# DeltaNet and a PReLU feed-forward block on one core: the opening with masked 16x16 blocks, half the columns, and values in three rounds

## The chip, the cores and the metric

The kernel runs on one core of one Trainium2 chip. The metric is device time in microseconds from the start to the end of one execution. Engines are called PE (TensorE), DVE (VectorE), ACT (ScalarE), POOL (GpSimd) and SP (SyncE, which here only issues loads and stores; its queue of them is SPq in the profile).

## The reference

Two blocks follow each other. The first is a delta rule over 768 tokens, for 4 batches and 8 heads of 48 dimensions, in float32:

```python
k_n = k / (norm(k) + 1e-06)
state = zeros((B, H, D, D))
for t in range(S):
    y[t] = q[t] @ state
    v_old = k_n[t] @ state
    state = state + beta[t] * outer(k_n[t], v[t] - v_old)
```

Its output, with the heads side by side as 3072 rows of 384, goes through the second block:

```python
h = x @ w_in                                   # 384 -> 2048
g = maximum(h, 0) + alpha * minimum(h, 0)
out = g @ w_out                                # 2048 -> 384
```

## The kernel before

The tokens are cut into 12 chunks of 64 (`C`). A step `n` is one chunk of one pair of batches, so there are 24 steps; steps 0 and 1 are chunk 0, steps 2 and 3 chunk 1. The 128 partitions of a step hold the 64 tokens of two batches. Inside a chunk the recurrence is a triangular system: with the weighted Gram matrix of the keys A (strictly lower), the values wanted are (I + A)^-1 times the values that the state leaves.

Most steps get that inverse from `eliminate`, which works on four steps (`NJ`) together with 32x32 blocks. The first four steps would wait too long for it. They use `eliminate_small`: it inverts only the 16x16 diagonal blocks (width `LB`, half of `HB`) on DVE, 14 dependent pairs of products and additions. What stands outside these blocks (`beyond`) is put in by a product: with own inverse D and outside part B, M = -DB is nilpotent (its fourth power is zero), so the inverse is (I + M)(I + M^2) D.

The opening of the program is, in this order, for steps 0 to 3:

- `squared`, `norms`: squares on ACT, sums on DVE. `flipped` (L412): keys turned by PE, copied by ACT to `k_t`.
- `grams` (L464): 16 products of 64x64 for each step; DVE multiplies them by the weights (L470) into three tiles: the columns of the own half (`same`), the other half (`right`), and `beyond` for steps 0 and 1. `keep` copies the second 32 rows; `outside` (L623 to L626) masks what stands outside the 16x16 blocks on ACT.
- `betas`, `slopes`: beta and alpha turned by PE (L316, L335). Alpha is loaded as `al_sb`; its slot is that of `prod`, which `eliminate_small` uses.
- `queries` (L1481): scores of q and k for chunk 0, masked by DVE (L1489).
- `short` and `busy` (L1474, L1466): matmuls whose results nobody reads; `busy(9)` runs beside the elimination. It reads `k_late[0]` (`kl`), the keys that the state update of step 0 also reads.
- `first_chunk`: `place_small` lays the inverses into 64x64 tiles (`own_inverse`); `matrices` makes M and its transpose and adds the identity (`eye`); `squared_matrix` M^2; three factors (L784 for all of these) give the values; then `outputs` (L857), `to_ffn` (L896: the outputs turned into the feed-forward block's operand).

The weights come in through a conversion of their own. `fetch_in` lets SP load pieces of w_in (128x512) into spare tiles (`stages`); `begin_in` runs two ACT instructions on a piece (L227, L229); `convert` adds one on DVE (L243) and one on POOL (L250). A piece's matmuls wait for the last.

`second_pair` does steps 2 and 3. Their products stand between the first-layer matmuls of chunk 0 (`ffn_in`, L995): `alongside(products, pieces)` puts so many of these matmuls and so many conversion halves behind a burst. Here `next_state` (L873) updates the state and `through_state` (L741, L729) reads it.

The order on each engine is written out by hand: `manual_schedule` keeps the order in which the program issues instructions, so an instruction that waits holds all behind it on its engine. SP's loads and stores go out in the order of the program as well. `hold` is a load of 4 bytes that makes SP wait for a tile. PSUM is shared out as three pairs of banks in turn (`ps_big`) and two banks for the feed-forward block (`ps_ffn`).

Of the kernel before, what the change touches and what calls it, by code (L numbers as in the profile page):

```python
# [32 lines left out]
C = 64  # L33
HB = 32
W_IN_P = 512
BUSY = 9.0
# [7 lines left out]
def kernel(  # L44
# [227 lines left out]
    eye = const.tile([128, C], FP32, name="eye")  # L272
    for t in range(2):
        nc.gpsimd.tensor_copy(out=minus[half(t)], in_=upper[half(t), half(t)])
    for t in range(2):
        nc.gpsimd.tensor_copy(out=eye[half(t)], in_=ident[half(t), half(t)])

    ones = work.tile([128, HB, HB], FP32, name="ones", tag="turned", bufs=1)
    nc.gpsimd.memset(ones, 0.0)
    nc.gpsimd.affine_select(  # L280
        out=ones, in_=ones, compare_op=ALU.is_ge, fill=1.0, base=0,
        pattern=[[1, HB], [-1, HB]], channel_multiplier=0,
    )
    inside_ = const.tile([128, HB * (HB + 1)], S8, name="inside")
    inside = inside_[:, 0 : HB * HB].rearrange("p (r c) -> p r c", c=HB)
# [3 lines left out]
    for t in range(2):  # L289
# [3 lines left out]
    first_of = const.tile([128, 1], FP32, name="first_of")  # L293
    nc.vector.tensor_reduce(
        out=first_of, in_=ident.rearrange("p (q u e) -> p u q e", u=2, e=HB // 2)[:, 0],
        axis=mybir.AxisListType.XY, op=ALU.add,
    )


    below = const.tile([128, 2], FP32, name="below")  # L300
    nc.gpsimd.tensor_tensor(out=below, in0=which, in1=first_of.to_broadcast([128, 2]), op=ALU.mult)
    nc.gpsimd.tensor_scalar(
        out=below[:, 0:1], in0=below[:, 0:1], scalar1=-1.0, scalar2=1.0, op0=ALU.mult, op1=ALU.add
    )
    nc.gpsimd.tensor_tensor(
        out=below[:, 1:2], in0=which[:, 1:2], in1=below[:, 1:2], op=ALU.subtract
# [42 lines left out]
    def zeros():  # L349

        for t in state:
            nc.scalar.memzero(t)

# [13 lines left out]
    ksq = {}  # L367

# [4 lines left out]
    def norms(n):  # L373
        stats[n] = work.tile([128, H], FP32, name="norm", bufs=EARLY + 3)
        nc.vector.tensor_reduce(out=stats[n], in_=ksq.pop(n), axis=AXX, op=ALU.add)  # L375
# [82 lines left out]
    def grams(n, p=None):  # L458

        if n >= N:  # L460
            return []
        p = region(p, G * C, g=G)
        for g, a, t in quarters():
            nc.tensor.matmul(  # L464
                p[half(t), a, g], k_t[n][dims(a), g, half(t)], k_t[n][dims(a), g, half(t)]
            )

        def weighted(dst, cols):
            w = stats[n][1][:, 0:2, :, None].to_broadcast([128, 2, G, HB])
            nc.vector.tensor_tensor(  # L470
                out=dst.rearrange("p (a g) i -> p a g i", a=2), in0=p[:, :, :, cols], in1=w,
                op=ALU.mult,
            )

        if n >= NJ:
            return [
                lambda: weighted(gather(n), slice(0, HB)),
                lambda: weighted(right[n % EARLY][:, 1:], slice(HB, C)),
                lambda: keep(n),
            ]  # L480
        return [
            lambda: weighted(gather(n), slice(0, HB)),
            lambda: weighted(right[n][:, 1:], slice(HB, C)),
            lambda: keep(n),
            lambda: weighted(beyond[n][:, :, 0:HB], slice(0, HB)),
        ]
# [13 lines left out]
    small = {}  # L500
    LB = HB // 2

    def own_blocks(flat):

        x = flat.rearrange("p (s e) -> p s e", s=2)[:, :, 0 : HB * LB]
        return x.rearrange("p s (r c) -> p s r c", c=HB)[:, :, :, 0:LB]

# [6 lines left out]
    def keep(n):  # L514

        m, j = n // NJ, n % NJ
        for t in range(2):
            own = slice(64 * t + HB, 64 * t + C)
            if n < FIRST + NJ and n != NJ - 1:
                nc.gpsimd.tensor_copy(out=same[m][own, j], in_=right[n % EARLY][own, 1:])  # L520
            elif n < NJ and t == 0:
                nc.vector.tensor_copy(out=same[m][own, j], in_=right[n % EARLY][own, 1:])
            else:
                nc.scalar.copy(same[m][own, j], right[n % EARLY][own, 1:])
        if (m, j) == (0, NJ - 1):
            for _ in turn_in(m):
                pass
# [11 lines left out]
    def turn_in(m):  # L539
        flat = work.tile([128, HB * (HB + 1)], FP32, name="block", bufs=1)  # L540
        block[m] = flat[:, 0 : HB * HB].rearrange("p (r c) -> p r c", c=HB)
        small[m] = own_blocks(flat)
        yield from turns(
            lambda x: block[m][:, x] if m == 0 else block[m][:, :, x].rearrange("b r c -> b c r"),
# [3 lines left out]
    def eliminate(m):  # L548

        if m > 0:  # L550
            yield from turn_in(m)
# [23 lines left out]
    def back(m):  # L575

        r = block[m]
        if m > 0:
            turned[m] = work.tile([128, NJ * H, HB], FP32, name="turned", bufs=1)
            yield from turns(  # L580
                lambda x: turned[m][:, :, x].rearrange("c b r -> c r b"), lambda x: r[:, x]
            )
# [10 lines left out]
    def eliminate_small(m):  # L593
        x = small[m]
        nc.vector.tensor_tensor(out=x, in0=x, in1=own_blocks(inside_), op=ALU.mult)
        yield
        for j in range(1, LB - 1):
# [12 lines left out]
            if j == 1:  # L610

                nc.gpsimd.memset(block[m][:, 0:LB, LB:HB], 0.0)
                nc.gpsimd.memset(block[m][:, LB:HB, 0:LB], 0.0)
                nc.gpsimd.memset(block[m].rearrange("p r c -> p (r c)")[:, :: HB + 1], 1.0)
            yield
        yield from back(m)

    def outside(n, part):

        x, left, last = beyond[n], beyond[n][:, :, 0:HB], right[n][:, 1:, 0:LB]  # L620
        if part == 0:
            src = left if n < 2 else same[0][:, n]
            nc.scalar.mul(left[:, :, 0:LB], src[:, :, 0:LB], below[:, 0:1])  # L623
            nc.scalar.mul(left[:, :, LB:HB], src[:, :, LB:HB], which[:, 1:2])
        else:
            nc.scalar.mul(x[:, :, HB : HB + LB], last, below[:, 1:2])  # L626
# [4 lines left out]
    def whole_block(out, x, i, by_vector=False):  # L631

        cols = slice(HB * i, HB * i + HB)
        if by_vector:
            nc.vector.tensor_scalar(
                out=out[:, :, cols], in0=x, scalar1=which[:, i : i + 1], scalar2=None, op0=ALU.mult
            )
        else:
            nc.scalar.mul(out[:, :, cols], x, which[:, i : i + 1])

    def place_small(n, by_vector):

        for i in range(2):
            whole_block(own_inverse[n], inverse[0][:, n * H : n * H + H], i, by_vector)
# [90 lines left out]
    def through_state(n, p=None, p_y=None):  # L735
# [9 lines left out]

        r = work.tile([128, 2, G, D], FP32, name="r")
# [3 lines left out]
        def less(to, own, a):  # L750
# [8 lines left out]
            *([lambda: weigh_rest_side(n)] if n < NJ else []),  # L759
# [4 lines left out]
    def weigh_rest_side(n):  # L764
        w = stats[n][1][:, 0:2, :, None].to_broadcast([128, 2, G, D])
        nc.vector.tensor_tensor(out=rhs_[n], in0=rhs_[n], in1=w, op=ALU.mult)

    def scale_first(n):
        c, bp = steps[n]
        nv[n] = v_raw.pop(n)  # L770
        nc.gpsimd.tensor_tensor(
            out=nv[n], in0=nv[n], in1=beta_t[:, c, bp, :, None].to_broadcast([128, H, D]),
            op=ALU.mult,
        )
        rhs_[n] = by_parity(nv[n])
# [4 lines left out]
    def crossing(out, x, y, back):  # L780

        for g, a, t in quarters():
            rows, own = (half(t ^ a), half(t)) if back else (half(t), half(t ^ a))
            nc.tensor.matmul(out[own, a, g], x[rows, a, g], y[rows, a, g])  # L784

    powers = {}

    def matrices(n, p=None):

        p = ps_big() if p is None else p  # L790
        one, other = (region(p[:, :, i * G * C : (i + 1) * G * C], G * C, g=G) for i in range(2))
        x, y = heads(own_inverse[n]), heads(beyond[n])
# [1167 lines left out]
```

## Time and profile before

| | us |
|---|---|
| median of 3 runs | 664.11 (663.17 to 664.46) |
| the profiled execution | 665.38 |
| its span, first to last instruction | 663.6 |
| PE: first instruction | 4.47 |
| DVE: the 14 steps of the small elimination | 19.85 to 27.64 |
| PE: first product of M | 31.09 |
| PE: first matmul of the feed-forward block | 47.92 |

Busy time of the engines in stretches of the opening (us, columns PE, weight loads, DVE, ACT, POOL each with the number of instructions, the granted clock of PE, the share of the DMA engines, GB/s):

```profile
20.00:30.00 10.00, 10.00 (x56) 4.81 (x49) 8.98 (x33) 7.86 (x18) 0.02 (x1) 1.00 1.07 340
30.00:40.00 10.00, 6.85 (x338) 5.47 (x336) 5.98 (x14) 4.54 (x9) 1.30 (x1) 1.00 0.63 113
40.00:50.00 10.00, 8.59 (x203) 7.27 (x203) 2.49 (x7) 6.18 (x13) 2.60 (x2) 0.83 0.57 170
```

A busy PE in the first of these is the filler. How to read a timeline line below: start, duration, engine, line of the kernel, operation, written tile and read tiles, shape, number of instructions; in brackets the idle time before it and what ended it. One float32 matmul of the program is two in the trace.

### The profile page before, as it was taken

The page shows a single profiled execution, that of the slowest core. Times are in us where ns is not written, and L with a number is a line of the kernel's source. Part 1 is how long each engine was busy: PE and PEld are TensorE (multiplying, and loading weights), DVE is VectorE, ACT ScalarE, POOL GpSimd, SP SyncE. Part 2 cuts the span into 40 slices and gives each one's busy share as a digit, 9 for nine tenths or more (in the row PEclk, how much of TensorE's full clock was granted, in tenths as well). Part 3 has the DMA queues.
Part 4 walks back from the last instruction along what each step waited for, and adds up shares of the span by engine and source line. Part 5 has one row for each costly group of instructions (what it writes and reads, how often), then busy time and mean ns, then how long its engine had stood idle before and what let it go on. Part 6 is the DMA issues. An engine that isn't in the chain of part 4 may idle for free.

```text
span 663.6 us, 21688 instructions
## 1 busy us (share of the span) xinstructions
PE 641.1 (97%) x9305; PEld 565.4 (85%) x9305; DVE 486.3 (73%) x1144; ACT 265.3 (40%) x620; POOL 124.6 (19%) x238
## 2 busy tenths in 40 slices
PE   6977998999999999999999999999999999999997
PEld 5566777656688988998998998988999999999997
DVE  4847479987899879758859748858968658568383
ACT  5755666424554252243343242232135235042140
POOL 6023554410010100001000000000035044052250
PEclk9989899999999999999999999999999999999999
DMA  7966555211342122122112112112111210100000
GB/s 118 290 151 126 154 140 134 74 36 29 65 80 50 27 52 46 26 49 50 26 38 37 27 38 37 26 39 37 26 41 35 41 34 3 28 11 2 25 0 25
DMA packets 111157, 37.68 MB, mean 57 GB/s; under 512 B 104230, under 2 KB 107446, under 8 KB 111062
## 3 DMA queue, kind: packets, MB, share of 16 engines
q1 hardware_dynamic: 109190, 35.81, 24.9%
q8 instruction: 73, 1.20, 0.7%
q10 hardware_dynamic: 1872, 0.49, 0.4%
q14 instruction: 22, 0.18, 0.1%
HBM read 31.56 MB, written 4.72 MB: 55 GB/s over the span
## 4 chain that ended last, share of the span: by engine, by line
PE 87%; DVE 7%; ACT 3%; issue 2%; DMA 1%; POOL 0%; SPq 0%; DVEq 0%; POOLq 0%; ACTq 0%
PE p_ffn L995 22%; PE p_ffn L1060 17%; PE p_more L1312 8%; PE p_ffn L1038 5%; PE p_more L1228 4%; PE p_ffn L1218 3%; PE p_ffn L1312 3%; PE p_ffn L1223 2%; PE p_pair L412 2%; PE p_pair L681 2%; PE p_pair L741 2%; PE p_pair L857 2%; PE p_pair L464 2%; PE p_pair L844 2%; PE p_pair L1466 2%
## 5 line engine op out<-in xcount | busy, mean ns | idle before, releaser
L995 PE MATMUL p_ffn<-xt,w_in 128*128 128x256 f32 x768 | 177.9, 385 | 3.2 <-DVE sums L1007 1.6
L995 PEld LDWEIGHTS p_ffn<-xt,w_in 128*128 128x128 f32 x768 | 142.7, 190 | 24.6 <-issue 2.3
L1007 DVE SCALAR_TENSOR_TENSOR act<-act,al_t,p_ffn 128x256 f32<-128x256 f32 x112 | 48.6, 475 | 23.8 <-ACT act L1005 23.6
L1005 ACT ACTIVATE act<-p_ffn 128x512 f32<-128x512 f32 x56 | 33.3, 595 | 79.1 <-PE p_ffn L995 78.9
L1252 POOL TENSOR_TENSOR k_t<-k_t 128x128 f32<-128x128 f32 (+1 forms) x48 | 28.9, 602 | 167.6 <-ACT k_t L1247 165.1
L569 DVE TENSOR_TENSOR block<-block,prod 128x30 f32<-128x30 f32 (+9 forms) x150 | 54.2, 361 | 5.2
L563 DVE TENSOR_TENSOR prod<-block 128x30 f32<-128x30 f32 (+9 forms) x150 | 52.0, 346 | 1.6
L401 POOL TENSOR_TENSOR beta_t<-beta_t,rec 128x8 f32<-128x8 f32 x24 | 5.9, 248 | 234.1 <-DVE rec L395 221.6
L1060 PE MATMUL p_ffn<-w_out,act 128*128 128x192 f32 x288 | 49.6, 328 | 0.0
L1060 PEld LDWEIGHTS p_ffn<-w_out,act 128*128 128x128 f32 x288 | 46.5, 190 | 0.3
L900 ACT COPY xt<-p_pair 128x384 f32<-128x384 f32 x22 | 10.4, 478 | 90.7 <-PE p_pair L896 76.9
L1252 POOL TENSOR_TENSOR block<-block 128x128 f32<-128x128 f32 (+1 forms) x48 | 27.6, 574 | 17.3 <-ACT block L1247 14.8
L1218 PE MATMUL p_ffn<-xt,w_in 128*128 128x256 f32 x96 | 28.7, 381 | 0.5 <-DVE o_sb L1080 0.5
L751 DVE TENSOR_TENSOR r<-v_raw,p_pair 64x192 f32<-64x192 f32 (+1 forms) x66 | 23.2, 352 | 2.2 <-PE p_pair L741 1.2
L693 ACT COPY inv<-p_pair 32x256 f32<-32x256 f32 x40 | 14.4, 361 | 24.9 <-DVE u L848 24.1
L1266 DVE SCALAR_TENSOR_TENSOR act<-block,al_t,act 128x256 f32<-128x256 f32 x32 | 19.7, 656 | 5.4 <-ACT block L1262 5.4
L733 ACT COPY y<-p_pair 128x384 f32<-128x384 f32 x22 | 10.4, 478 | 32.4 <-PE p_pair L729 30.8
L1080 DVE TENSOR_TENSOR o_sb<-u,p_ffn 128x192 f32<-128x192 f32 x24 | 7.9, 351 | 20.5 <-PE p_ffn L1060 20.1
L1266 DVE SCALAR_TENSOR_TENSOR act<-k_t,al_t,act 128x256 f32<-128x256 f32 x32 | 22.3, 734 | 0.1
L375 DVE TENSOR_REDUCE norm<-ksq 128x8 f32<-128x384 f32 x24 | 12.9, 547 | 12.7 <-ACT ksq L371 12.6
L1247 ACT COPY k_t<-p_more 128x512 f32<-128x512 f32 x16 | 9.4, 586 | 31.4 <-PE p_more L1228 26.7
L1312 PE MATMUL p_more<-w_out,act 128*128 128x192 f32 x128 | 21.9, 329 | 0.0
(276 smaller groups left out, 1429.6 us busy)
## 6 DMA issues: line engine op xcount, KB each, us to landing
qp<-in_q_dram SPq DMA_DIRECT2D x48, 96.0 KB, 3.2
v_raw<-in_v_dram SPq DMA_DIRECT2D x48, 96.0 KB, 2.6
kl<-in_k_dram SPq DMA_DIRECT2D x96, 48.0 KB, 2.6
out_dram<-o_sb SPq DMA_DIRECT2D x90, 48.0 KB, 1.6
space_out<-in_moe_w_out_dram SPq DMA_DIRECT2D x11, 384.0 KB, 3.2
ke<-in_k_dram SPq DMA_DIRECT2D x43, 96.0 KB, 2.8
w_out<-in_moe_w_in_dram SPq DMA_DIRECT2D x7, 512.0 KB, 8.4
w_out<-in_moe_w_out_dram SPq DMA_DIRECT2D x5, 384.0 KB, 6.0
```

The lines of the kernel that those rows point to most:

```text
L563: nc.vector.tensor_tensor(out=prod, in0=r[:, 0:j, j : j + 1].to_broadcast([128, j, n]), in1=r[:, j : j + 1, j + 1 : HB].to_broadcast([128, ...
L569: nc.vector.tensor_tensor(out=r[:, 0:j, j + 1 : HB], in0=r[:, 0:j, j + 1 : HB], in1=prod, op=ALU.add)
L995: nc.tensor.matmul(p_h[:, i], w_in[:, t, (f + i) * 128 : (f + i + 1) * 128], xt[:, t], start=(t == 0), stop=(t == KT - 1),)
L1005: nc.scalar.activation(g, p_h, ACT.Relu, scale=-1.0)
L1007: nc.vector.scalar_tensor_tensor(out=g[:, i], in0=g[:, i], scalar=al_t[:, f + i : f + i + 1], in1=p_h[:, i], op0=ALU.mult, op1=ALU.add,)
L1038: nc.tensor.matmul(p_o[u], gs[f // 2][:, f % 2, u * 128 : (u + 1) * 128], w_out[:, f], start=(f == 0), stop=(f == FT - 1),)
L1060: nc.tensor.matmul(p, x(i), w(i), start=(i == 0), stop=(i == FP - 1))
L1218: nc.tensor.matmul(p[:, f * 256 : f * 256 + 256], w(2, f), xt[:, 2], start=True, stop=False)
L1228: nc.tensor.matmul(q[:, j], a, b, start=True, stop=True)
L1252: nc.gpsimd.tensor_tensor(out=dst, in0=a, in1=b, op=ALU.add)
L1266: nc.vector.scalar_tensor_tensor(out=g[:, f], in0=r[:, f], scalar=al_t[:, 2 * i + f : 2 * i + f + 1], in1=g[:, f], op0=ALU.mult, op1=ALU.add,)
L1312: nc.tensor.matmul(p, x(i), w(i), start=(i == 0), stop=(i == FP - 1))
```

## The change

The opening of steps 0 to 3 is written anew; the rest of the program keeps its order.

- Gram products of these steps put heads with odd index on the other 64 rows (`half(t ^ a)`) and leave PSUM unweighted. `pick` takes the own 16 columns of each row by four masks (`quarter_of`), one on ACT and three on DVE; `raw` copies the first 48 columns to `beyond`. The weights come as tiles, `own_weight` and `below_weight` (mask times weight, made on POOL by `first_weights` for two steps at once); `weigh_own` (DVE) and `weigh_below` (POOL) apply them. `keep`, `outside`, `ones`, `inside`, `eye` go.
- `eliminate_small` turns two tiles in and two out instead of four and four.
- `matrix` makes one M (one group of 16 products instead of two) and no square. The values come in rounds: z = Dv, u = z + Mz, r = z + Mu, result = z + Mr, each a group of products and an addition on DVE. For odd heads a round needs rows on the other half: `turn_matrix` and `turn_values` make copies, on ACT or POOL.
- `scale_first` (POOL) now is three instructions for each of the four steps and writes a tile of its own. `queries` are copied by ACT and masked by POOL.
- `busy` 9 to 6, `short` gone, the states zeroed on POOL early, the `hold` loads gone. All 12 pieces of w_in have a tile of their own. Pieces are loaded earlier: four ahead of v, two ahead of alpha, two ahead of the late keys; six are begun on ACT before the values instead of four. Keys of steps 5 and 6 are turned in `second_pair`.

```diff
-BUSY = 9.0
+BUSY = 6.0
...
+            own = half(t ^ a) if n < NJ else half(t)
             nc.tensor.matmul(
-                p[half(t), a, g], k_t[n][dims(a), g, half(t)], k_t[n][dims(a), g, half(t)]
+                p[own, a, g], k_t[n][dims(a), g, half(t)], k_t[n][dims(a), g, half(t)]
...
+    def pick(n, p, q):
+        src, dst = p[:, :, :, q * LB : q * LB + LB], own_part[:, n]
+        if q == 0:
+            nc.scalar.mul(dst, src, quarter_of[:, 0:1])
+        else:
+            nc.vector.scalar_tensor_tensor(
+                out=dst, in0=src, scalar=quarter_of[:, q : q + 1], in1=dst, op0=ALU.mult, op1=ALU.add
+            )
...
+    def place_small(n, by_vector):
...
+            for q in range(NQ4):
+                nc.scalar.mul(out[:, :, q], x, quarter_of[:, q : q + 1])
...
+    def turn_values(n, engine):
+        z, turned_z = by_parity(nv[n]), step_space(n)[2]
+        copy_by(engine, turned_z[:, 0], z[:, 0])
+        swapped(engine, turned_z[:, 1], z[:, 1])
+
+    def one_round(n, i, p):
...
+        src, add, dst = (
+            (z, turned_z, u), (u, z, rhs_[n]), (rhs_[n], turned_z, us.get(n)),
+        )[i]
+        crossing(p, [m[:, 0], turned_m if i == 1 else m[:, 1]], src, i == 1)
+        return [lambda: nc.vector.tensor_tensor(out=dst, in0=add, in1=p, op=ALU.add)]
...
     for n in range(2):
         load_q(n)
+    fetch_in(4)
+    for n in range(2):
         load_v(n)
-    load_late(0)
+    fetch_in(6)
     nc.sync.dma_start(out=al_sb, in_=moe_alpha.rearrange("(f p) -> f p", p=128))
-    fetch_in(n_in)
...
+    fetch_in(8)
+    raw(2, gram_2)
+    raw(3, gram_3)
+    slopes()
...
+    load_late(0)
     load_late(1)
...
     mask = queries()
+    weigh_below(1)
...
     busy(BUSY)
-    begin_in(3)
+    begin_in(6)
+    eliminate_small()
...
+        now(matrix(0, ps_big()[:, :, 0 : G * C]))
+        convert(2)
+        z_0 = own(0)
+        m_1 = matrix(1, ps_big()[:, :, 0 : G * C])
+        now(z_0)
+        turn_values(0, nc.gpsimd)
+        now(m_1)
+        z_1 = own(1)
         convert(1)
+        now(z_1)
+        turn_matrix(0, nc.scalar)
+        turn_values(1, nc.scalar)
+        convert(1)
+        turn_matrix(1, nc.scalar)
+        for i in range(3):
+            rounds = [round_(n, i) for n in both]
+            for x in rounds:
+                now(x)
...
+        burst(matrix, G * C)
         for i in both:
-            scale_v(i)
+            turn_matrix(i, nc.gpsimd)
+        alongside(2, 2)
...
+        burst(own_values, G * D)
+        for i in both:
+            turn_values(i, nc.gpsimd)
...
-        burst(third_factor, G * D)
+        burst(lambda i, p: one_round(i, 2, p), G * D)
```

## The prediction

> **What bounds the kernel now.** I read the page's busy totals and slices first, then the chain of waits from 0 to 130 us, then what TensorE (PE) waited for, then the timelines of PE, ScalarE (ACT) and the load queue (SPq) in that stretch.
>
> ```profile
> PE 641.1 (97%) x9305; PEld 565.4 (85%) x9305; DVE 486.3 (73%) x1144; ACT 265.3 (40%) x620; POOL 124.6 (19%) x238
> PE   6977998999999999999999999999999999999997
> ...
> 19.05 1.98 PE p_ffn L1481 x64
> 21.04 10.12 PE p_pair L1466 x18
> 31.16 1.14 PE p_pair L784 x64
> ...
> PE p_pair L784 <- issue: 2.8, 2, 1.8
> ...
> PE p_pair L784 <- ACT sums L803: 2.7, 1, 2.7
> ```
>
> PE is full except in the first slices of 16.6 us. So the time is PE's work plus what the opening leaves idle, and a microsecond gained there is kept, because behind it PE always has work. Three landmarks in PE's own order: the filler (`busy`, L1466) runs 20.97 to 31.16; the first feed-forward matmul (L995) starts at 47.92; the transposes of the second pair's outputs (`to_ffn`, L896) start at 85.79. From that last point on PE's instructions are the same in both programs, one for one. So the forecast is: where does 85.79 go?
>
> **Loads: what the moved pieces stand in front of.** The SPq timeline and the DMA counts of 18 to 27 us and of 27 to 31 us:
>
> ```profile
> 19.17 5.17 SPq L161 DMA_DIRECT2D kl<-in_k_dram  x4
> ...
> DMA packets 991, 3.64 MB, mean 405 GB/s; under 512 B 108, under 2 KB 108, under 8 KB 987
> ...
> DMA packets 2224, 0.57 MB, mean 142 GB/s; under 512 B 2183, under 2 KB 2183, under 8 KB 2224
> ```
>
> Four short-row loads were issued from 19.17 on, behind eight w_in pieces; almost no short packet moved until the pieces were through at 27. One queue serves its loads in order. SPq's own waits on landings (issues at 20.61, 22.37, 23.63, 25.81, 27.09) put the pieces 1.6 us apart. Short loads of 512 packets went at 871 packets per us (1742 in 8 to 10 us), 0.585 us each.
>
> After, SPq has q, then four w_in pieces, v, two pieces, **the alpha load (al_sb)**, two pieces, then kl for step 0. Before, alpha was ahead of every piece (issue 14.26, on PE by 16.34). After: the 12 short loads end at about 9.5 us (4812 of 6144 packets by 8.0, the rest at 871 per us), six pieces 9.6, v's four loads 2.3: alpha lands at about 21.4. PE's transpose of alpha (L335) stands ahead of the q transposes, the queries and the filler, so all of these wait. Two pieces (3.2) and four half-size loads (1.2) later, at 25.8, kl lands, which the filler reads. Lower bound for alpha, if it were not in order: issue after the third piece (14.9) plus the 1.9 it took before, 16.8; upper, a slowest ring late by one more piece, 23.
>
> **Removed or moved, and hidden.** Gone from POOL by 8 us are `ones` (0.95 + 1.26), two `eye` copies (0.51) and three small products; new there are the zeroing of the states (about 0.4 each by the 0.95 for 1024 columns; 0.93 off ACT) and `first_weights` (per chunk four small products at 0.27, one of 256 columns at about 0.55, one of 64 at 0.25), done by 11.4 and 14.6, before their readers on DVE. Twelve `outside` products (0.3 to 0.4) and two `same` copies leave ACT; eight picks and raw copies (0.31 and 0.48) come, done by 16.5. `short` (1.48) leaves PE. All of this lies ahead of the wait for alpha, so its saving is covered by that wait; without it the elimination alone would come 4 us sooner. The three `hold` loads (0.61 to 0.73 of SPq's time each) go; the last four w_in pieces are issued before 37 instead of at 38 to 54, ahead of v for step 3, which POOL's scaling of step 3 reads at 45 by my count, when that load has just landed (44.5).
>
> **The opening up to the values.** PE: 16.34 to 20.97 took 4.63 from L335 to the end of the queries, so after: 21.5 + 4.6 = 26.1. Filler, 12 instructions instead of 18: it starts with the slow clock as before (five at 0.85, then 0.43), 4.3 + 7 x 0.43 = 7.3, so 33.4.
> VectorE (DVE): Gram products without the weighting first, picks (three per step at about 0.31, between 0.28 for L607 at 128x112 and 0.44 for L1007 at 128x256), two transposes of 0.53 instead of four in and two instead of four out (saves 2.2), no `inside` product (0.69). I get the elimination's start at 16.5 instead of 19.85; its 14 steps are the same 7.8. It pauses at its seventh step for the alpha buffer (to 21.5) and ends at 25.9, then stands until POOL's memset of ones, which is queued behind `mask` (two 128x512 products, 1.1 to 1.3 each by L771 and L250) and so behind ACT's copies of the queries: 29.5. Inverse ready 30.6 instead of 29.82.
> ACT: two copies of the queries 1.1, `minus` 0.3, then `begin_in(6)`: six pairs at 1.26 (22.10 to 23.36), 7.56, where before three ran ahead; then `place_small(1)`, four quarter products 0.29 apart, 1.2. From 26.2: **36.4**. This is last: the filler is done at 33.4, DVE at 31.3. So ACT takes over, and the filler's missing third is worth nothing.
>
> **From there to the first feed-forward matmul**, along what ends last: matrix(1) 0.7, its copy 0.55, `turn_matrix(0)` on ACT two half copies 0.75 (L524: 0.40), `turn_values(1)` three copies 0.9, round-0 add 0.55, a conversion between (L243) 0.4, the two round-1 adds 1.1 on DVE, of which 0.55 hides, round 2 0.65 and adds 1.15, `outputs` behind one key flip 0.95, copy 0.6, transposes 0.55, xt copy 0.55: 8.9. Before, 16.8 lay between filler and L995, with twelve groups of 16 products, ACT and DVE taking turns on one PSUM tile, and 2.8 of "issue" (PE stopping in the middle of a group; a 16 KB packet of the instruction queue moved at 34 and at 38, at the same times). After there are ten groups; I charge 1.6 for such stops and slow clock together (0 to 3.4). 36.4 + 8.9 + 1.6 = 46.9: **1.0 gained** at this landmark.
>
> ```profile
> 61.48 1.13 PE L995 MATMUL p_ffn<-xt,w_in 128*128 128x256 f32 x4
> ...
> 65.98 0.84 PE L784 MATMUL p_pair<-sums 64*64 64x64 f32 x32 [2.66 <-ACT sums L803]
> 66.75 2.07 PE L995 MATMUL p_ffn<-xt,w_in 128*128 128x256 f32 x4
> ```
>
> What slow clock costs stands here: after a gap of 2.66, four L995 take 2.07 instead of 1.13, and 65.98 to 70.28 holds 2.3 us of work. PE's gap behind the filler in the new opening is about 2 to 3. The Trainium skill, "TensorE: Matmul & The Clock Gate", section "What's actually happening", has the clock halve after a whole idle window of about 3.4 us; by that rule this gap might leave it full and the 1.6 would shrink, while the row shows that 2.66 was enough. The sum goes by the row.
>
> **The second pair, 47.92 to 85.79 (37.9).** Work: 38 first-layer matmuls at 0.465 (97.66: twelve half-instructions in 2.8), 17.7; twelve groups at 0.48, 5.8; state reads 2.6; three flips 1.3; next_state, Grams, outputs 2.8: 30.2. So 7.7 is waiting and slow clock: 2.7 for ACT's copies of the matrices (queued behind weight conversions), 2.0 slow clock behind it, 1.0, 0.4, and 1.6 in small pieces. After: ten groups and five flips, again 30.1. By the queues I find a wait of 1.15 (flip NJ+1 needs the PSUM that ACT's y copies read) and one of 1.25 (round 1 behind DVE's conversions, the slopes and the round-0 adds), each too short for slow clock; with 1.0 for the rest, 33.5. **4.3 gained**; bounds 0 (all waits come back) to 6.5. POOL gets 2.7 + 1.8 + 2.7 more here (scaling v, `turn_matrix`, `turn_values`), covered by its idle time (23.5 busy in 50 to 100). Unknown are its copies of 64 partitions to the other half: 0.25 (L402) to 1.3 (L250); nearest L520 (32x256, 0.41), so 0.43.
>
> Sum: 1.0 + 4.3 = 5.3. The profiled run took 665.38 (span 663.6), so 660.1; the median shown, 664.11, is 1.27 lower, so **658.8** for the median.
>
> **Rivals.**
> A, alpha and kl do not wait for the whole queue. Speaks for it: alpha is 8 KB in 16 rows and took 1.9 before. Against: the short loads at 19.17. Then ACT's chain ends 4.5 earlier and the gain is 9.8: 654.3. The Trainium skill, "DMA: Bandwidth & Descriptors", section "Queues, rings and completion order", says that completion is not in issue order for one engine, a small transfer on few rings may finish earlier; the packet counts cannot exclude it for alpha.
> B, the waits come back: ACT still holds the conversions ahead of the matrix copies in the second pair, so 2.7 + 2.0 and the rest return. For it: ACT does eight more quarter products there. Gain 1.0: 663.1, about no change.
> C, slower: **POOL becomes the bound of the second pair.** Place: scaling, `turn_matrix`, `turn_values` stand between its weight additions (1.30 each), and the round-0 adds wait for them. Eight half copies and four half products; at 1.3 instead of 0.43 they add 10.4, of which POOL's slack before round 0 takes about 3. 7.4 - 5.3: 2.1 slower, 666.2. It decides from 0.43 + 8.3/12 = 1.1 each. Against: L520.
> D, the change does less than it says, by the filler: if kl lands after 30, the filler ends after ACT; each microsecond more is lost. It needs 2.5 pieces more in the queue than I count; with kl at 33, 662.8.
>
> **Chances.** Forecast 0.48 (gains 2 to 8), A 0.18, B 0.14, C 0.16, D 0.04. This kernel's measurement tells changes from about 0.2%, 1.3 us. Faster: 0.48 + 0.18 + 0.05 of B + 0.02 of D = 0.73; same 0.09 of B and 0.02 of D = 0.11; slower: C 0.16. Range 653.5 to 666.0: A at one end, C nearly at the other; the likeliest alone 656 to 662.
>
> **What would show it.** L335's successor at 21 to 22 us with an idle PE from 14 on (A: at 17); the last quarter product of `place_small(1)` at 36, after the filler's end; the first feed-forward matmul near 47; the second pair's `to_ffn` near 80.5; no gap over 1.5 in between. Wrong if POOL's half copies take a microsecond, if PE stands over 2.5 before round 1, or if the stretch from there to the end is not as long as before (577.8 of span).

## The result, and the profile after

| | us | runs |
|---|---|---|
| before, median | 663.90 (660.96 to 665.03) | 20 |
| after, median | 665.25 (662.88 to 668.67) | 20 |
| after / before | 1.0028, 95% interval 1.0014 to 1.0041 | |
| profiled execution before / after | 665.38 / 662.88 | |
| their spans | 663.6 / 661.1 | |

The change makes the kernel 0.28% slower, a little more than the 0.2% that can be told from no change; on another chip (the run e1 below) it was 0.16%, which does not exclude no change. Forecast were 658.8 and 0.73 for faster: wrong. The two profiles alone would say 2.5 us faster, but the one of after is of its fastest execution. So two more profiles of before and two of after were taken (among the experiments), and the tables below use them. First the page of after, the lines that answer to those shown of before: busy time by engine, and PE's busy tenths in 40 slices.

```profile
PE 632.1 (96%) x9147; PEld 560.7 (85%) x9147; DVE 483.4 (73%) x1140; ACT 261.3 (40%) x610; POOL 136.7 (21%) x258
...
PE   5569998999999999999999999999999999999997
```

PE has 9.0 us less work than before, so the change took out what it meant to take out. The first two slices went from 6 and 9 tenths to 5 and 5: the removed work came back as idle time ahead of 33 us. PE's timeline of after from the transpose of alpha to the first feed-forward matmul:

```profile
23.61 0.26 PE L335 MATMUL p_pair<-ident,al_sb 16*128 16x16 f32 x1 [9.16 <-DMA al_sb<-in_moe_alpha_dram]
...
27.98 5.39 PE L1534 MATMUL p_pair<-kl,ident 128*128 128x512 f32 x12 [0.33 <-DMA kl<-in_k_dram]
33.96 0.69 PE L852 MATMUL p_pair<-inv,sums 64*64 64x64 f32 x32 [0.59 <-DVE inv L698]
...
37.78 1.13 PE L852 MATMUL p_pair<-inv,sums 64*64 64x64 f32 x32 [2.67 <-ACT inv L704]
...
42.23 0.53 PE L852 MATMUL p_pair<-act 64*64 64x48 f32 x12 [0.21 <-DVE act L907]
44.61 0.77 PE L852 MATMUL p_pair<-act 64*64 64x48 f32 x19 [1.85 <-issue]
...
51.33 1.10 PE L1070 MATMUL p_ffn<-xt,w_in 128*128 128x256 f32 x4
```

PE waits 9.16 for alpha, then 2.67 until ACT has placed the second step's inverse (`place_small(1)`, L704). The matrix behind that wait takes 1.13 where the first took 0.69. In the middle of a group PE stops for 1.85 with no wait shown. VectorE's and GpSimd's timelines of the same execution, the end of the elimination:

```profile
31.72 1.18 DVE L652 STREAM_TRANSPOSE inverse<-block 128x256 f32<-128x256 f32 x2 [3.34 <-POOL block L681]
```

```profile
29.09 2.50 POOL L1559 TENSOR_TENSOR a_t<-a_t,minus 128x512 f32<-128x512 f32 x2 [6.13 <-ACT minus L1733]
31.53 0.15 POOL L681 MEMSET block<- 128x32 f32 x1
```

VectorE had its last step done at 28.4 and stood 3.34 for a fill of 0.15, because the two mask products of `queries` (L1559) were ahead of it in GpSimd's queue.

A second execution of after took 665.75, near the median (the run e15 below). The two lines of PE that differ most from the first one:

```profile
28.38 8.06 PE L1534 MATMUL p_pair<-kl,ident 128*128 128x512 f32 x12 [0.41 <-DMA kl<-in_k_dram]
...
45.54 0.77 PE L852 MATMUL p_pair<-act 64*64 64x48 f32 x19 [2.94 <-issue]
```

Its 12 filler matmuls took 0.86 each in the median instead of 0.59, and the stop was 1.1 longer. The landmarks of all profiles of the two kernels, in us; "first product" is the first of M, "second pair" runs from the first feed-forward matmul to the transposes of its outputs, "rest" from there to the end of the span:

| execution | alpha's transpose | filler ends | first product | first FFN matmul | second pair | rest |
|---|---|---|---|---|---|---|
| before, 665.38 | 16.34 | 31.16 | 31.09 | 47.92 | 37.87 | 577.8 |
| before, 664.99 (e13) | 16.22 | 29.41 | 30.12 | 47.86 | 37.22 | 578.2 |
| before, 665.05 (e14) | 16.14 | 29.81 | 30.39 | 47.14 | 38.35 | 577.8 |
| after, 662.88 | 23.61 | 33.37 | 33.96 | 51.33 | 32.95 | 576.8 |
| after, 664.62 (e1) | 24.35 | 33.77 | 34.71 | 52.27 | 33.73 | 576.9 |
| after, 665.75 (e15) | 23.91 | 36.44 | 36.37 | 53.05 | 34.17 | 576.8 |

Executions of after differ by 2.9 us of span, and all of it lies ahead of the transposes at 84.3 to 87.2. The second pair gained what was forecast: on the average of three profiles each, 4.2. The opening lost 4.6, and the rest gained 1.1. By these profiles after would be 0.7 shorter. The 1.35 by which its median is longer is therefore not located: all three profiles of before are of executions above their median.

### The profile page after: what moved, and what is told of

Same layout as the page of the kernel before. It is cut to its first block, busy times and chain, and to the rows that moved or that the text cites. A ratio compares the mean times of both kernels' runs of the same rounds, so it can differ in the third digit from the quotient of the medians.

```text
span 661.1 us, 21374 instructions
## 1 busy us (share of the span) xinstructions
PE 632.1 (96%) x9147; PEld 560.7 (85%) x9147; DVE 483.4 (73%) x1140; ACT 261.3 (40%) x610; POOL 136.7 (21%) x258
## 3 DMA queue, kind: packets, MB, share of 16 engines
q8 instruction: 72, 1.18, 0.7%
## 4 chain that ended last, share of the span: by engine, by line
PE 86%; DVE 5%; ACT 4%; SPq 2%; DMA 1%; issue 1%; POOL 0%; ACTq 0%; DVEq 0%; POOLq 0%
PE p_ffn L1070 22%; PE p_ffn L1135 17%; PE p_more L1387 8%; PE p_ffn L1113 5%; PE p_more L1303 5%; PE p_ffn L1293 3%; PE p_ffn L1387 3%; PE p_pair L416 3%; PE p_pair L801 2%; PE p_ffn L1298 2%; PE p_pair L741 2%; PE p_pair L925 2%; PE p_pair L912 2%; PE p_pair L852 2%; PE p_pair L472 2%; PE p_pair L789 1%
## 5 line engine op out<-in xcount | busy, mean ns | idle before, releaser
L820 DVE TENSOR_TENSOR r<-v_raw,p_pair 64x192 f32<-64x192 f32 (+1 forms) x60 | 21.2, 353 | 2.2 <-PE p_pair L801 1.2
L949 DVE TENSOR_TENSOR beside<-beside,p_pair 48x384 f32<-48x384 f32 (+1 forms) x36 | 19.8, 549 | 2.9 <-PE p_pair L941 2.7
L1113 PE MATMUL p_ffn<-w_out,act 128*128 128x384 f32 x64 | 21.6, 490 | 0.0
```

What stands on the lines that cost most here:

```text
L1113: nc.tensor.matmul(p_o[u], gs[f // 2][:, f % 2, u * 128 : (u + 1) * 128], w_out[:, f], start=(f == 0), stop=(f == FT - 1),)
```

## The experiments

Theories, as the expectations name them. T1: the load order (alpha, then the late keys) holds the opening. T2: ACT's six conversions, the stops and the slow clock set it whatever is loaded first. T3: the loss lies behind the second pair. Later ones are T-queue (what stands ahead of the inverse on GpSimd and ScalarE), T-ACT, T-clock, T-stops and T-stream (PE's stops), T-share (VectorE is slowed by GpSimd), T-base and T-end. Ratios are against runs of before on the same chip.

| run | edit | median us (n) | ratio to before, 95% interval |
|---|---|---|---|
| e1 | after, unedited | 665.13 (12) | 1.0016 (0.9997 to 1.0035) |
| e2 | after, alpha first | 664.39 (12) | 1.0012 (0.9994 to 1.0031) |
| e3 | after, alpha and late keys first | 661.43 (12) | 0.9957 (0.9935 to 0.9979) |
| e4 | before, alpha behind six pieces | 670.55 (6) | 1.0093 (1.0071 to 1.0115) |
| e5 | after, masks later, three conversions | 662.48 (12) | 0.9985 (0.9964 to 1.0007) |
| e6 | e3, masks later | 657.83 (6) | 0.9895 (0.9874 to 0.9916) |
| e7 | e3, masks later, three conversions | 658.49 (6) | 0.9909 (0.9881 to 0.9938) |
| e8 | e3, three conversions | 662.58 (12) | 0.9974 (0.9955 to 0.9992) |
| e9 | after, nine units of filler | 666.00 (12) | 1.0032 (1.0014 to 1.0050) |
| e10 | e6, eight units of filler | 661.84 (10) | 0.9959 (0.9934 to 0.9984) |
| e11 | e6, second pair's weighing later | 657.28 (6) | 0.9898 (0.9867 to 0.9928) |
| e12 | e7 with e11's edit, eight units | 657.31 (6) | 0.9888 (0.9868 to 0.9908) |
| e16 | after, three units of filler | 664.11 (12) | 0.9999 (0.9983 to 1.0014) |

### The load order: e1 to e4

```diff
     for n in range(2):
         load_q(n)
+    nc.sync.dma_start(out=al_sb, in_=moe_alpha.rearrange("(f p) -> f p", p=128))
+    load_late(0)
     fetch_in(4)
...
     fetch_in(6)
-    nc.sync.dma_start(out=al_sb, in_=moe_alpha.rearrange("(f p) -> f p", p=128))
...
-    load_late(0)
     load_late(1)
```

This is e3; e2 moves the first of the two loads alone; e4 is the kernel before with alpha's load put behind six pieces of w_in.

> The changed kernel once more, unedited, beside the kernel before. Every theory expects 665.2 (663 to 668) and the same landmarks within 2 us: alpha's transpose at 23.6, first product of M at 34 and its second half at 37.8, first feed-forward matmul at 51.3, the second pair's output transposes at 84.3. What differs between this profile and the first one is the spread that no theory may use.

> The changed kernel with the alpha load ahead of every w_in piece. Theory 1 (the load order holds the opening: alpha, then the late keys): alpha's transpose at 16 to 16.5, queries done by 21, ACT's last quarter product at 31 instead of 37.7, but the filler still waits for the late keys (27.6) and ends at 33 to 35, so the products of M go on at 34 to 35 instead of 37.8; first feed-forward matmul 48 to 49; 2.5 to 4 us faster than the changed kernel, 661 to 663. Theory 2 (ACT's six conversions ahead of the quarter products, stops and slow clock set the opening, wherever the load stands): the first feed-forward matmul within 1 of 51.3, the time within 1 of the changed kernel. Theory 3 (the loss lies behind the second pair): the landmarks move and the time does not.

> Alpha and the late keys of step 0 both ahead of every w_in piece. Theory 1: filler from 21 to 27 or 28, ACT's last quarter product at 31 to 32, first feed-forward matmul 44 to 46; 5 to 7 us faster than the changed kernel, 658 to 660, so faster than the kernel before by 4 to 6. Theory 2: within 1 of the changed kernel. Theory 3: landmarks move, time stays near 665.

> The kernel before with its alpha load put behind the first six w_in pieces, nothing else. Theory 1: alpha lands at 26 to 27, queries done at 31, filler 31 to 41, first product of M at 41 instead of 31.1; 8 to 11 us slower than before, 672 to 675. Theory 2: within 1 of the kernel before.

In e4 alpha's transpose came at 26.27 instead of 16.1 to 16.3 and the kernel lost 6.6: alpha's place in the queue is a real price on its own, though not one to one (ten late, 6.6 lost; T1 had 8 to 11). In e2 the transpose is at 16.41, and the time hardly moves, where T1 had 661 to 663. PE's timeline of e2 shows why:

```profile
28.98 8.28 PE L1534 MATMUL p_pair<-kl,ident 128*128 128x512 f32 x12 [8.49 <-DMA kl<-in_k_dram]
```

The filler reads the late keys, which lie behind the same pieces. PE idles 8.49 for them instead of 9.16 for alpha, and the filler, which took 5.39 in the first profile of after, takes 8.28, so the first product of M stands at 37.19. Only when both are early (e3) is there a gain, 2.5 us on before and 3.7 on after, where T1 had 5 to 7: the filler now ends at 27.8 and PE idles 3.98 for VectorE. T3 falls: the rest took 576.8 to 576.9 in all three of e1, e2 and e3.

### What stands ahead of the inverse: e5 to e8

```diff
     for i in range(2):
         scale_first(i)
-    mask()
...
     busy(BUSY)
-    begin_in(6)
+    begin_in(3)
     eliminate_small()
...
         turn_matrix(1, nc.scalar)
+        mask()
         for i in range(3):
```

e6 has the mask's move alone, e8 the three conversions alone, e7 both, each on e3; e5 is both without the load order.

> The changed kernel with two edits behind the filler and the load order left as it is: the masks of A (2.50 us of GpSimd) are issued after the fourth turn of the first pair, and three weight conversions instead of six stand ahead of the elimination on ScalarE. T-queue (what stands on GpSimd and ScalarE ahead of the inverse): VectorE's wait of 3.34 for GpSimd's fill of ones goes, the inverse is ready at about 29.4 instead of 32.9, ScalarE's four placing copies end before the filler does at 33.4, the wait of 2.67 ahead of the second matrix goes and with it part of the slow clock: 660.5 (658.5 to 662). T1 (alpha behind the six weight pieces holds the opening): the filler still ends at 33.4 and only the 0.5 ahead of the first matrix is won: 664.5.

> The kernel with alpha and the late keys loaded first, and the masks of A issued after the fourth turn of the first pair; six conversions stay. T-queue, GpSimd's part: VectorE's last elimination steps (0.5 to 1.3 us each from 22 to 30 while GpSimd worked, 0.2 to 0.3 in the profile of before) take a half of that, at least from the place where the masks stood, the inverse is ready at about 27.5 instead of 30.9, the first matrix stands right behind the filler at 28 and the idle 3.98 goes: 658 (656 to 660). T-ACT: ScalarE is bound by its six conversions to 29.2 and its four placing copies to 30.5, so the second matrix starts there instead of at 32.3: 659.5. T-stops (fixed stops of PE in the rounds and the slow clock set the time whatever is early): 661.4.

> The same with three conversions instead of six ahead of the elimination. T-queue with both parts: ScalarE is free at 25.3, its placing copies follow the inverse at 27.5 and end at 28.8, all four matrix groups run behind the filler with no wait above 0.5, and the clock stays full: 656.5 (654 to 658.5). If only GpSimd's part counts: as the kernel with the masks alone (658). T-stops: 661.4.

> The kernel with alpha and the late keys first, the masks where they were, and three conversions instead of six. T-queue: ScalarE waited 1.80 for the inverse in the kernel it is made from, so it is not last and nothing is won: 661.4, or up to 1.5 more where the three conversions moved back come in the way of the first pair's copies. T-ACT: 1.3 to 3 us won, 658.5 to 660.

The mask's place is worth 3.6 us on e3 (661.43 to 657.83; ratios 0.9957 and 0.9895, measured on two chips), as T-queue said for GpSimd's part. The conversions are worth nothing on e3, as it said for e8, and nothing on e6 either (e7), where it had 1.5. VectorE's timeline of e3, late steps of the elimination with the masks running from 25.42 to 27.86:

```profile
21.82 0.27 DVE L669 TENSOR_TENSOR prod<-block 128x108 f32<-128x108 f32 x1
...
23.20 0.53 DVE L675 TENSOR_TENSOR block<-block,prod 128x100 f32<-128x100 f32 x1
...
25.46 1.32 DVE L675 TENSOR_TENSOR block<-block,prod 128x72 f32<-128x72 f32 x1
26.82 1.17 DVE L669 TENSOR_TENSOR prod<-block 128x52 f32<-128x52 f32 x1
```

GpSimd scales values from 21.92 and masks from 25.42 (its timeline has these two as 3.42 and 2.50). VectorE's steps, 0.27 before, take 0.53 and then 1.2 to 1.3. In the profile of before the same steps took 0.23 and 0.21, with GpSimd idle. So the masks cost in two ways, one in each kernel. In after the elimination was over before they began, and they delayed the fill of ones. In e3 the fill was in time (27.86, with the last step ending at 29.86), and they stretched the elimination. PE's timeline of e6 at the same place:

```profile
29.92 1.13 PE L852 MATMUL p_pair<-inv,sums 64*64 64x64 f32 x32 [2.87 <-DVE inv L698]
...
43.95 2.07 PE L1070 MATMUL p_ffn<-xt,w_in 128*128 128x256 f32 x4
```

The first feed-forward matmul stands at 43.95, 7.4 to 9.1 earlier than in the three profiles of after. The second pair then takes 35.66 instead of 33 to 34; in it GpSimd waits 8.20 for the values of step 3, which may be why. Of the gain over e3 only 1.9 stands at the first product of M (31.78 in e3). From there to the first feed-forward matmul the two profiles differ by 4.2 more, 2.5 of it in PE's stops (1.07 and 2.74 in e3, 0.15 and 1.14 in e6). So 3.6 is what the move was worth with the stops as they fell, and not the price of the masks alone. e5 gains some 2 to 3 on after without the load order, less than the 4.7 that T-queue had: there the filler, at 28.59 to 36.26, was last.

### The length of the filler, and PE's stops: e9, e10, e16

```diff
-BUSY = 6.0
+BUSY = 9.0
```

> The changed kernel with one number changed: nine units of filler instead of six (18 matmuls of 128x512, of 0.45 each at full clock). T-clock (PE's idle 2.67 ahead of the second matrix is what lowers the clock for the next 10 us): the filler ends at about 36.1 instead of 33.4, the second matrix still starts at 37.8 when ScalarE has placed it, but the groups behind it run at full length (0.65 to 0.7 for 32 instead of 1.0 to 1.1) and the first pair is some 2 to 3 us shorter: 662.5 (661.5 to 663.5). If the slow clock costs nothing because the chain hangs on VectorE and ScalarE anyway: 665.2 or a little more.

> The changed kernel with three units of filler instead of six, so six matmuls fewer. T-stream (the stops without a wait stand at fixed places of PE's own instruction stream, and what is saved ahead of them comes back as a longer stop): the stop of 1.85 that stood 12 matmuls into a group of the first round, and 6 into it with six matmuls more, stands 18 into it; it is short, because PE waited before it, and the time stays within 1 of 665. T-clock: PE idles some 6 us ahead of the second matrix instead of 2.67, the slow clock holds longer, and the time is 1 to 2 us more.

> The kernel with alpha and the late keys first and the masks moved, with eight units of filler instead of six. T-clock: the idle 2.87 ahead of the first matrix becomes about 1, the matrix starts where it did (29.9, VectorE sets it), the four groups behind it take 0.65 to 0.7 instead of 0.95 to 1.13: 1.5 us, 656.3 (655 to 657.5). Otherwise 657.8; later than that if the filler runs past the inverse.

T-clock fails as a price of its own. e9 took the wait of 2.67 away and every group behind it ran at full length, yet the time did not fall. The filler did run past ScalarE, to 37.8, so that the second matrix began at 38.71, 0.9 later than in after. But from there to the first feed-forward matmul it took 13.55, exactly as in after with its slow groups (37.78 to 51.33); the stop was longer. The two lines of e9, then of e16, from PE's timeline: the stop.

```profile
42.62 0.32 PE L852 MATMUL p_pair<-act 64*64 64x48 f32 x6 [0.46 <-DVE act L907]
45.45 0.61 PE L852 MATMUL p_pair<-act 64*64 64x48 f32 x26 [2.50 <-issue]
```

```profile
41.31 1.86 PE L852 MATMUL p_pair<-act 64*64 64x48 f32 x50
45.40 0.57 PE L852 MATMUL p_pair<-act 64*64 64x48 f32 x12 [2.23 <-issue]
```

The second of the two groups of round 1 (32 matmuls each) is cut 6 matmuls in with 18 filler matmuls, 12 in with 12 (the profile of after above), and 50 - 32 = 18 in with 6. The cut moves by exactly the number added or taken ahead of it: it is a place in PE's own instruction stream. It also ends at about the same time, 45.45, 44.61 to 45.66, and 45.40. That does not make the time a fixed one: in all of these PE had come to the place 128 matmuls earlier at about the same time as well, at 39.3, 38.9 to 39.7, and 39.0. Where it came there sooner, the stop ended sooner: 37.9 and 43.50 in e5, 34.7 and 42.33 in e3. In e13, a profile of before, two cuts stand one after the other:

```profile
35.46 0.45 PE L784 MATMUL p_pair<-v_raw,act 64*64 64x48 f32 x17 [1.12 <-issue]
35.73 0.83 PE L784 MATMUL p_pair<-act 64*64 64x64 f32 x32
36.32 1.07 PE L784 MATMUL p_pair<-v_raw,act 64*64 64x48 f32 x32
37.15 1.12 PE L784 MATMUL p_pair<-act 64*64 64x64 f32 x32
38.02 0.64 PE L784 MATMUL p_pair<-r,act 64*64 64x48 f32 x15
39.63 1.62 PE L784 MATMUL p_pair<-r,act 64*64 64x48 f32 x49 [0.96 <-issue]
```

17 + 32 + 32 + 32 + 15 = 128 matmuls lie between them, each with a weight load: 256 instructions. The page of after has this queue in its list (packets, MB, share):

```profile
q8 instruction: 72, 1.18, 0.7%
```

72 packets of 16 KB; PE's 2 x 9147 matmuls and loads make 71.5 blocks of 256. One such packet began to move at 42.35 in after, at 43.25 in e15, 43.07 in e16 and 43.09 in e9, and at 33.00 and 37.34 in e13; PE went on 2.3 to 2.5 after each. So the stop is PE waiting for its next block of instructions, and T-stream's place of it is shown. The Trainium skill, "Runtime: NRT & Kernel Launch", section "Instruction fetch mechanics", says that each engine's instructions are refilled in blocks of 16 KB, 256 instructions, by its own queue, and calls the crossing mostly hidden; the count of 256 agrees, and here up to 3.4 us of a crossing (e8) are not hidden.

The same packets show from when a stop has to be counted. Each moved only after PE had begun the block before: 0.9 to 1.9 after it at the two stops in the profiles of before, 3.4 to 4.4 after it in those of after, e9 and e16. From the beginning of one block to that of the next PE took 3.3 to 4.5 there and 5.6 to 6.7 here; where the block's own work takes less, the difference is a stop. What makes a packet late isn't shown. While PE waited for the late ones the DMA engines moved 301 to 391 GB/s, with the last four pieces of w_in on their way, which after issues at 35.42 to 37.98 and before at 38.34 to 53.87; in before they moved 110 to 137. But another block of before came after 1.5 with 291 GB/s moving, and no run moved these four loads alone.

T-stream's expectation that the stop in e16 would be short did not hold (2.23), and its time was right. That what is saved ahead of a stop comes back in it is not tested by e16: PE stood for ScalarE until 37.7 in both kernels. e10 gave 661.84 with runs from 656.68 to 664.77, where 656.3 or 657.8 was expected, and worse than e6 by 4 us; its own profile, of a run of 657.4, has the idle time at 1.04 as expected and a stop of 2.62 in the block in front. Why its other runs are slower stays open.

### GpSimd beside VectorE, and all together: e11, e12

```diff
-    for n in range(2, NJ):
-        weigh_below(n)
...
         mask()
+        for n in range(2, NJ):
+            weigh_below(n)
```

> The kernel with alpha and the late keys first and the masks moved, with GpSimd's weighing of the second pair's blocks (1.7 us for two) issued behind the masks as well, so that during the elimination GpSimd has only the scaled values. T-share (a step of VectorE's elimination takes twice its time or more while GpSimd works): the last four steps take 0.21 instead of 0.74, the transposes less, the inverse is ready 1.5 earlier, at 27.5, and the second pair does not wait for its blocks: 656.5 (655.5 to 657.5). If the long steps have another cause they stay at 0.5 to 0.7: 657.8.

> All of it together: alpha and the late keys first, the masks and the weighing of the second pair's blocks behind the first pair's turns, three conversions ahead of the elimination, eight units of filler. If the parts add up: inverse at 27.5 to 28.5, filler up to there, no slow clock behind it: 655 (653.5 to 657). If the load order and the masks are all there is: 657.8.

VectorE's timelines of e6 and then of e11, the last steps; GpSimd's weighing runs from 26.02 to 27.73 in e6 and at 35.5 in e11, its scaling of values until 25.9 in both:

```profile
27.03 0.74 DVE L669 TENSOR_TENSOR prod<-block 128x28 f32<-128x28 f32 x1
...
27.92 1.12 DVE L652 STREAM_TRANSPOSE inverse<-block 128x256 f32<-128x256 f32 x2
```

```profile
25.49 0.51 DVE L669 TENSOR_TENSOR prod<-block 128x52 f32<-128x52 f32 x1
26.03 0.21 DVE L675 TENSOR_TENSOR block<-block,prod 128x52 f32<-128x52 f32 x1
26.28 0.20 DVE L669 TENSOR_TENSOR prod<-block 128x28 f32<-128x28 f32 x1
...
26.63 1.14 DVE L652 STREAM_TRANSPOSE inverse<-block 128x256 f32<-128x256 f32 x2
```

T-share holds: the same step takes 0.74 beside GpSimd's work and 0.20 without it, and the change from 0.51 to 0.21 stands where GpSimd's scaling ends. The transposes, which read one tile, took 1.18 beside the same weighing in after (31.72, above) and 1.1 here, where GpSimd was done. The Trainium skill, "SBUF — State Buffer", section "SBUF: two separate sides", has a port pair that VectorE's operations with two inputs in SBUF and GpSimd's take in turn; these rows agree with it. The inverse is ready 1.29 earlier (1.5 expected), but the time is the same as e6's (0.9898 and 0.9895): behind it PE waits 0.63 for ScalarE's placing, the two stops grew from 0.15 and 1.14 to 0.51 and 1.33, and the first feed-forward matmul stands at 44.08 instead of 43.95. e12 has the parts together and no more than e6, where 655 was expected if they add up: from 0.9888 to 0.9909 e6, e7, e11 and e12 cannot be told apart. They beat both kernels, before by 5 to 7 us.

### More profiles of the two kernels: e13 to e15

> The kernel before, unedited, for a second profile of it. Its first profile was of an execution of 665.4, which is 1.3 above the median of its runs. T-base (the profile that the prediction was worked from showed the opening too late): in an execution of 662 to 664 the first FFN matmul stands 1 to 3 us earlier than the 47.92 that was read, and the stretch from L896 at 85.8 to the end is as long as it was (577.8). T-end: the opening is the same to 0.5 and the rest of the kernel is what differs.

> The kernel before, unedited, for a third profile. T-base: first FFN matmul 1 to 3 us earlier than 47.92 in an execution of 662 to 664, and the stretch behind L896 as long as it was (577.8). T-end: the opening the same to 0.5, the rest differs.

> The changed kernel, unedited, for a third profile of it (executions of 662.9 and 664.6 so far, with the first FFN matmul at 51.3 and 52.3). T-base: in a run of 665 to 666 it stands 2 to 3 later than 51.3, with a longer stop of PE in the rounds or a later alpha, and the stretches behind it are the same to 0.5.

Both executions of before fell near 665 again, with the opening within 0.8 and the rest within 0.4 of the first, so whether a run of 662 has an earlier opening wasn't seen, and T-base is not shown for before. For after it holds in part: e15's first feed-forward matmul stands 1.7 later than in the first profile (2 to 3 expected), its second pair took 1.2 more (0.5 at most expected), and the rest is the same to 0.1.

## Why the prediction was wrong

It forecast 46.9 and 33.5 for the two stretches up to the second pair's transposes, 80.4 in all. The profiles have 84.3, 86.0 and 87.2. Step by step, with the first profile of after and e15:

- **Alpha at 21.4.** Right in kind (not early, as rival A had it), short by 2.2 to 2.5. The step counted when the queue serves, not when the load is issued: the load queue's timeline of after, below, has alpha issued only at 19.00, because the issues ahead of it take 4.37 and 4.17. From 17.6 to 18.9, while they held it up, the queue moved hardly anything (16 to 76 GB/s). It was in use 4.6 later.

```profile
10.37 4.37 SPq L137 DMA_DIRECT2D v_raw<-in_v_dram  x4
14.78 4.17 SPq L210 DMA_DIRECT2D w_out<-in_moe_w_in_dram  x2
19.00 0.43 SPq L1668 DMA_DIRECT2D al_sb<-in_moe_alpha_dram  x1
```

- **Filler 7.3, to 33.4.** 5.39 and 8.06, to 33.4 and 36.4. That the first agrees to the tenth is luck: it began 1.9 later than forecast and took 1.9 less. The granted clock is given as 1.00 for both, so what made the second slower isn't shown.
- **VectorE's wait for the fill behind the masks, inverse at 30.6.** Right in kind; 32.9 and 33.2. Its price was put at nothing because ACT was to be later. That held in after; with the loads early PE waits for VectorE (3.98 in e3, 2.87 in e6), though there not for the fill.
- **ACT last, at 36.4.** 37.7 and 38.0, and PE waits 2.67 and 0.55 for it: right, 1.3 to 1.6 late by alpha's lateness.
- **The chain, 8.9 + 1.6, bounds 0 to 3.4 on the second term. This is the term that failed most.** It took 51.33 - 37.72 = 13.6 and 53.05 - 38.01 = 15.0, which is 4.7 and 6.1 above the 8.9. PE's one stop is 1.85 and 2.94 of that; the other 2.9 and 3.2, slow clock and links longer than forecast, were not taken apart. The granted clock of after by windows (busy time of PE, weight loads, VectorE, ACT and GpSimd, then the clock, the DMA share and GB/s):

```profile
37.80:39.00 1.20, 1.20 (x46) 1.20 (x48) 0.00 (x0) 0.42 (x2) 0.61 (x1) 0.50 0.68 157
39.00:41.00 2.00, 2.00 (x76) 1.89 (x76) 0.83 (x2) 1.91 (x5) 0.00 (x0) 0.50 0.98 377
...
46.00:48.00 2.00, 2.00 (x75) 2.00 (x67) 1.19 (x3) 0.00 (x0) 1.43 (x3) 0.50 0.09 20
```

  The clock was halved twice, behind the wait of 2.67 and behind the stop of 1.85. The forecast took 2.8 of stops from the profile of before and let the change shrink them, since it takes groups away. But a stop belongs to a block of 256 instructions and is counted from the beginning of the block before, not from the groups. There is one stop here instead of two, but it stands in a step from block to block of 5.6 to 6.7 us, against 3.3 to 4.5 in before. So taking groups away did not shorten the stretch: from the first product of M to the first feed-forward matmul, before took 16.8, 17.7 and 16.8, and after 17.4, 17.6 and 16.7, with fewer groups of products. The forecast had 13.5 there (33.4 to 46.9); the 3.3 to be saved came back whole.
- **Second pair 33.5, 4.3 gained.** 32.95, 33.73 and 34.17: right. Of its two waits one came, 1.0 for ACT's y copies where 1.15 was forecast. The 1.25 ahead of round 1 did not; in its place PE had stops of 0.7 to 1.6 in all. So the closeness of the sum is in part luck.
- **Rest as long as before, 577.8.** 576.8: 1.0 less, not forecast; its cause wasn't sought.
- **Base.** The forecast took 1.27 off for a profile above the median. For before that stands; after's median lies 2.4 above its own profile.

So, with e14 and e15, which are both near 665: first feed-forward matmul 5.9 later (47.14 to 53.05), second pair 4.2 shorter, rest 1.0 shorter, together 0.7 on the span. The miss against the forecast, 665.25 - 658.8 = 6.5, is the chain and what leads to it, 4.4 to 6.2 at its end, of which alpha's and ACT's lateness is 1.3 to 1.6.

The rivals: A and B did not happen. C was to be slower by GpSimd in the second pair; its half copies are 0.41 each (two in 0.83), so the size excludes it. GpSimd did cost something in the first pair instead, by its queue and, with the loads early, by VectorE's slower steps. D named the late keys, and they were next in line (e2), at 28 and not at 33. None of the rivals had the case that came, in which the opening takes back the second pair's gain, so the 0.16 for slower stood on the wrong mechanism.

## What to carry to other kernels

A small load that the first work of an engine needs has to be issued ahead of the large ones, and all such loads together: moving alpha alone moved the wait to the late keys. Short GpSimd work that seems free, like the masks, is to be priced by what is queued behind it and by VectorE's two-input steps that run beside it: here moving 2.5 of such work was worth 3.6 us, stops of PE included. And stops of PE that stand 128 matmuls apart belong to blocks of its instructions: a saving inside a block of small matmuls should be counted only down to the time that PE needs from one block to the next, 3.3 to 6.7 us in these profiles.

## What the runs showed of the hardware

- PE's instructions arrive in blocks of 256 (128 matmuls with their loads, 72 packets of 16 KB in the whole program), and in a stretch of small matmuls PE stopped up to 3.4 us at such a border (e8); the border moves one for one with matmuls put ahead of it. The packet of a block began to move 0.9 to 1.9 us (before) or 3.4 to 4.4 us (after) after PE had begun the block before it, and PE went on 2.3 to 2.6 us later.
- The clock was halved after gaps of 2.67 and 1.85. The Trainium skill, "TensorE: Matmul & The Clock Gate", section "What's actually happening", gives a whole idle window of about 3.4 us for that; here shorter gaps were enough.
- A VectorE product with two tiles took 0.20 to 0.28 alone, 0.5 beside GpSimd's scaling (128x192), 0.74 beside its weighing (128x384), and 1.2 to 1.3 beside its 128x512 products.
